# Two of the three transpose groups of a batch moved together, and both halves of a small product moved behind the last Newton step

## The chip, the cores and the metric

The kernel runs on one core of one Trainium2 chip. The metric is the device time of one execution in microseconds (us); for a kernel it is the median over its runs. The kernel before took 1432.73 us, the median of three runs between 1431.31 and 1433.15.

## What is computed

The reference chains a Nystrom attention and two feed-forward blocks. For each of 8 batches and 8 heads, with 576 positions of 64 channels, q and k are averaged over groups of 18 positions to 32 landmarks, and

```python
A = sm(q, k_lm); Bm = sm(q_lm, k_lm); C = sm(q_lm, k)     # row softmax of scaled products
Z = Bm.T / (norm1(Bm) * norminf(Bm) + 1e-06)
for _ in range(6):
    Z = 2 * Z - Z @ Bm @ Z                                # Newton steps
attn = A @ Z @ C @ v
x = ((attn @ w1) * (attn @ w2)) @ w3 @ w_out              # first block
out = elu(x @ w_in) @ w_out2                              # second block
```

The change touches only how C @ v is scheduled: the exponentials of C's scores have to be transposed before they can be multiplied with v.

## The kernel before

The work falls into three stretches. A start-up prepares the first batch and folds w3 and w_out into one matrix. Then comes the attention and first-block stretch, from about 130 to 640 us of the profile: 128 units, 16 for each of 8 batches. A last stretch computes the second block. The change lies in the middle one.

A unit `u` of batch `b` has two half steps, numbered `hs` = 0 to 31 within the batch. In each unit the loop at L915 issues, in this order: `ab(u)` (12 TensorE matmuls, L707 to L709), `quick` (the `r0` or `newton` step of the even half step, if there is one, L890), `ab_product(u)` (a ScalarE copy L716 and a VectorE product L718), the split of the product of the unit before (ScalarE L70, VectorE L71), `fill` for the even half step, `yy(u - 2)` (12 matmuls, L734 to L736), and `fill` for the odd half step. The order is written out by hand, and every engine works through its own instructions in this order.

`fill(b, hs)` runs, among other things, the attention steps of the *next* batch that the table `steps` (L522) has under `hs`. So the attention of batches 1 to 7 is computed piecewise between the matmuls of the batch before. Batch 0 has a table of its own (`first=True`) and is computed in the start-up.

The steps that matter here, for batches 1 to 7:

- `c_scores` at 7 and 8 writes the raw scores of C into two tiles `e` (128 partitions by 576, one for each half of the heads). `c_max` and `c_exp` at 9 and 10 take the maximum (VectorE L334, L335) and the exponential in place (ScalarE L338): the half 0 at 9, the half 1 at 10.
- `b_norms` at 10 and `b_norms2` at 11 prepare the Newton iteration on VectorE; `b_norms2` ends with the product at L399. `r0` at 12 (issued by `quick`) is 8 small matmuls (L406) and one VectorE product out of PSUM (L408). `newton` at 13 to 18 is six times 8 small matmuls (L418) and one VectorE operation out of PSUM (L420). Each depends on the one before.
- `c_trans` (L423) comes in three parts. Part 0 transposes four 128-column blocks of `e[0]` on TensorE (L429) into one PSUM tile, and ScalarE copies this to `ct` (L434). Part 1 does the same for `e[1]`. Part 2 transposes the last 64 columns of both halves (L432), copied by L436.
- `cv` (L438) multiplies `ct` with v, 20 matmuls (L447) for each half into one PSUM tile; after the second half VectorE scales the result into `cvbd` (L457). `zcv` at 21 (L466) multiplies it with the Newton result, and `m_tiles` (24 to 3 of the next batch, L317 with `z`) uses that. `a_scores` (22 and 26) and its steps on VectorE (L488 and on) are the other half of the attention.

All PSUM tiles of these steps come from one pool with two buffers, taken in turn:

```python
ps_at = ctx.enter_context(tc.tile_pool(name="ps_at", bufs=2, space=bass.MemoryType.PSUM))   # L243
def ps(self, nm):
    return ps_at.tile([128, 512], F32, name=f"{nm}_{self.b}", tag="at")                      # L290
```

A matmul into a new tile has to wait until the tile that last held this buffer has been read out. In the kernel before the order of tiles is, from half step 11 on: transposes 0, r0, Newton 0, transposes 1, Newton 1, Newton 2, transposes 2, Newton 3, 4, 5, cv, z.

Of the kernel before, what the change touches and what calls it, by code (L numbers as in the profile page):

```python
# [64 lines left out]
def nystrom_moe_kernel(ctx, tc, qT, kT, vm, vr, w12, w3T, w_out1, w_in2, w_out2, out):  # L65
# [216 lines left out]
    class Attention:  # L282
# [239 lines left out]
        def steps(self, first=False):  # L522

            s = {}

            def at(i, f, *a):
                s.setdefault(i, []).append((f, a))

            for hp in range(NP):
                at((-16, -14, -12, -11)[hp], self.sums, "k", hp)  # L530
                at(hp, self.sums, "q", hp)
            at(4, self.q_pad)
            lead = 2 if first else 0
            at(6 - lead // 2, self.b_scores)
            at(7 - lead // 2, self.b_exp)
            if first:
                at(7, self.b_soft)
                at(7, self.c_scores, 0)
                at(8, self.b_norms)
                at(8, self.c_scores, 1)  # L540
                at(9, self.b_norms2)
            else:
                at(7, self.c_scores, 0)
                at(8, self.c_scores, 1)
                at(8, self.b_soft)
            at(9, self.c_max, 0)
            at(9, self.c_exp, 0)
            if not first:
                at(10, self.b_norms)
            else:  # L550
                at(10, self.r0)
            at(10, self.c_max, 1)
            at(10, self.c_exp, 1)
            if not first:
                at(11, self.b_norms2)
                at(12, self.r0)
            at(17 if first else 13, self.c_norm)
            for k in range(6):
                at(13 - lead + k, self.newton, k)
            for k in range(3):  # L560
                at(11 + lead // 2 + 2 * k, self.c_trans, k)
            at(18, self.cv, 0)
            at(19, self.cv, 1)
            at(21, self.zcv)
            when = ((22, 22, 23, 24, 25, 26, 27), (26, 27, 28, 29, 30, 32, 34))
            if first:
                when = ((11, 11, 12, 13, 14, 15, 16), (17, 17, N1, N1 + 1, N1 + 2, N1 + 3, N1 + 4))
            for n, o in enumerate(when):
                at(o[0], self.a_scores, n)
                at(o[1], self.a_max)  # L570
                at(o[2], self.a_sub)
                at(o[3], self.a_exp)
                at(o[4], self.a_sum)
                at(o[5], self.a_mul, n)
                at(o[6], self.a_split, n)
            return s
# [6 lines left out]
    with tc.manual_schedule():  # L583
# [55 lines left out]
        for o in ORDER:  # L639
            if o == "A":  # L640
                k, n_wo = n_wo, n_wo + 1
# [400 lines left out]
```

## Time and profile before

| What | Value |
|---|---|
| Median of 3 runs (1431.31 to 1433.15) | 1432.73 us |
| The profiled execution: span from first to last instruction | 1430.4 us |
| Its own time beside the span | not given apart; the three runs lie 0.9 to 2.8 us above this span |
| TensorE (PE) busy | 1368.1 us, 96% |
| VectorE (DVE) busy | 1087.5 us, 76% |
| ScalarE (ACT) busy | 630.4 us, 44% |
| GpSimd (POOL) busy | 367.7 us, 26% |
| Mean granted TensorE clock | 0.988 of full speed |

PE is the matmul engine, and PEld its loads of weights, which overlap the matmuls. In a timeline a row has its start, its length, the engine, the line of the kernel, the operation, what it writes and reads, and how many neighbours were merged into it; a square bracket gives how long the engine sat idle before it and what ended that. The ends of matmuls are modelled, so the distance from one start to the next tells more than the length. An fp32 matmul leaves two records, so that 8 matmuls read x16 and 20 read x40.

### The profile page before, as it was taken

How to read it: one execution, taken by the hardware profiler on the slowest of the kernel's cores; microseconds unless marked ns; L12 is line 12 of the kernel's file. 1: busy time of each engine (PE TensorE's matmuls, PEld its weight loads, DVE VectorE, ACT ScalarE, POOL GpSimd, SP SyncE). 2: the span in 40 equal slices, each digit the busy share in tenths (PEclk: the TensorE clock that was granted, in tenths of full speed). 3: DMA queues.
4: the chain of work that ended last, by engine and by line, in shares of the span. 5: the costliest groups of instructions: out<-in, count | busy, mean ns of one | idle time of the engine just before them, and what ended most of it. 6: DMA issues, size and time to landing. Idle time of an engine off the chain costs nothing.

```text
span 1430.4 us, 27132 instructions
## 1 busy us (share of the span) xinstructions
PE 1368.1 (96%) x10848; PEld 1178.8 (82%) x10848; DVE 1087.5 (76%) x2003; ACT 630.4 (44%) x1266; POOL 367.7 (26%) x378
## 2 busy tenths in 40 slices
PE   5786999999999999999999999999999999999998
PEld 2234788888878888899999989999898998989987
DVE  7988687778687787744887878878687887878774
ACT  5534454445344545433444443544443444434442
POOL 4442336345265363420301101010110101011000
PEclk9988999999999999999999999999999999999999
DMA  8744354453535543252976464565646556555440
GB/s 306 239 139 132 109 168 164 158 179 101 203 99 195 200 136 112 93 201 81 416 259 220 155 247 173 198 221 184 224 166 222 198 185 226 193 199 192 179 159 30
DMA packets 56014, 259.70 MB, mean 182 GB/s; under 512 B 5200, under 2 KB 14416, under 8 KB 43600
## 3 DMA queue, kind: packets, MB, share of 16 engines
q0 software_dynamic: 12672, 140.51, 27.2%
q1 hardware_dynamic: 43216, 117.46, 23.7%
q8 instruction: 85, 1.39, 0.4%
q14 instruction: 41, 0.34, 0.1%
HBM read 216.01 MB, written 41.94 MB: 180 GB/s over the span
## 4 chain that ended last, share of the span: by engine, by line
PE 84%; DVE 12%; DMA 2%; ACT 1%; issue 1%; SPq 0%; DVEq 0%; ACTq 0%
PE o L873 9%; PE o L872 9%; PE o L871 9%; PE hm L812 8%; PE hm L813 8%; PE hm L814 8%; PE y L734 5%; PE ab L707 4%; PE ab L708 4%; PE ab L709 4%; PE y L736 4%; PE y L735 4%; PE m L317 2%; DVE w_b L128 1%; DVE w_b L124 1%
## 5 line engine op out<-in xcount | busy, mean ns | idle before, releaser
L812 PE MATMUL hm<-yb,wh 128*128 128x256 f32 x1008 | 285.2, 283 | 2.5 <-DVE g L830 1.7
L813 PE MATMUL hm<-yb,wh 128*128 128x256 f32 x1008 | 285.1, 283 | 0.0
L814 PE MATMUL hm<-yb,wh 128*128 128x256 f32 x1008 | 284.9, 283 | 0.0
L873 PE MATMUL o<-wo,el 128*128 128x512 f32 x576 | 225.6, 392 | 0.0
L872 PE MATMUL o<-wo,eh 128*128 128x512 f32 x576 | 225.3, 391 | 0.0
L871 PE MATMUL o<-wo,eh 128*128 128x512 f32 x576 | 224.0, 389 | 0.0
L843 ACT ACTIVATE t<-m 128x512 f32<-128x512 f32 x144 | 89.9, 624 | 299.3 <-DVE m L841 299.3
L812 PEld LDWEIGHTS hm<-yb,wh 128*128 128x128 f32 x1008 | 192.9, 191 | 5.7 <-DVE g L830 1.9
L758 POOL DMA_DIRECT2D wh<-wh_d x72 | 39.4, 548 | 611.0 <-PE hm L814 606.4
L813 PEld LDWEIGHTS hm<-yb,wh 128*128 128x128 f32 x1008 | 192.9, 191 | 2.8
L814 PEld LDWEIGHTS hm<-yb,wh 128*128 128x128 f32 x1008 | 193.0, 192 | 0.0
L734 PE MATMUL y<-gh,w3oh 128*128 128x288 f32 x512 | 160.8, 314 | 2.9 <-DVE w3ol L71 2.9
L846 DVE SCALAR_TENSOR_TENSOR t<-m,t 128x512 f32<-128x512 f32 x144 | 99.2, 689 | 77.9 <-ACT m L844 77.9
L707 PE MATMUL ab<-ath,mh 128*128 128x288 f32 x512 | 157.1, 307 | 0.0
L708 PE MATMUL ab<-atl,mh 128*128 128x288 f32 x512 | 151.9, 297 | 0.0
L709 PE MATMUL ab<-ath,ml 128*128 128x288 f32 x512 | 151.3, 295 | 0.0
L736 PE MATMUL y<-gh,w3ol 128*128 128x288 f32 x512 | 151.2, 295 | 0.0
L735 PE MATMUL y<-gl,w3oh 128*128 128x288 f32 x512 | 151.0, 295 | 0.0
L734 PEld LDWEIGHTS y<-gh,w3oh 128*128 128x128 f32 x512 | 96.3, 188 | 40.7 <-issue 22.3
L873 PEld LDWEIGHTS o<-wo,el 128*128 128x128 f32 x576 | 108.1, 188 | 22.6
L871 PEld LDWEIGHTS o<-wo,eh 128*128 128x128 f32 x576 | 108.5, 188 | 20.9
L872 PEld LDWEIGHTS o<-wo,eh 128*128 128x128 f32 x576 | 108.1, 188 | 21.2
(146 smaller groups left out, 2729.5 us busy)
## 6 DMA issues: line engine op xcount, KB each, us to landing
wh<-wh_d POOLq DMA_DIRECT2D x72, 1792.0 KB, 7.8
wo_raw<-in_w_out_dram SPq DMA_DIRECT2D x24, 512.0 KB, 5.3
k<-in_kT_dram SPq DMA_DIRECT2D x8, 1152.0 KB, 7.1
q<-in_qT_dram SPq DMA_DIRECT2D x8, 1152.0 KB, 5.2
yd<-ysb SPq DMA_DIRECT2D x16, 576.0 KB, 3.6
yin<-yd SPq DMA_DIRECT2D x9, 1024.0 KB, 9.9
out_dram<-osb SPq DMA_DIRECT2D x36, 256.0 KB, 2.3
w_raw<-in_w3T_dram SPq DMA_DIRECT2D x16, 512.0 KB, 5.1
```

What stands on the lines that cost most here:

```text
L707: pe.matmul(p[:, :NH], mh[:, cs], ah[:, blk, :], start=(blk == 0), stop=False)
L708: pe.matmul(p[:, :NH], mh[:, cs], al[:, blk, :], start=False, stop=False)
L709: pe.matmul(p[:, :NH], ml[:, cs], ah[:, blk, :], start=False, stop=(blk == 1))
L734: pe.matmul(a[oc][:, :NH], w3o_hi[fc][:, os_], gh, start=(fc == 0), stop=False)
L735: pe.matmul(a[oc][:, :NH], w3o_hi[fc][:, os_], gl, start=False, stop=False)
L736: pe.matmul(a[oc][:, :NH], w3o_lo[fc][:, os_], gh, start=False, stop=(fc == K1 - 1))
L812: pe.matmul(o, ah, bh[:, kk, :], start=(kk == 0), stop=False)
L813: pe.matmul(o, ah, bl[:, kk, :], start=False, stop=False)
L814: pe.matmul(o, al, bh[:, kk, :], start=False, stop=(kk == 1))
L871: pe.matmul(a, eh[:, ts_], w[:, 0, :], start=first, stop=False)
L872: pe.matmul(a, eh[:, ts_], w[:, 1, :], start=False, stop=False)
L873: pe.matmul(a, el[:, ts_], w[:, 0, :], start=False, stop=last)
```

## The change

For batches 1 to 7, part 0 of the transposes stays at half step 11, part 1 moves from 13 to 12, and part 2 from 15 to 12. The first half of the product with v moves from 18 to 19, where the second half already is. For batch 0 the numbers stay what they were (12, 14, 16 and 18).

```diff
             for k in range(3):
-                at(11 + lead // 2 + 2 * k, self.c_trans, k)
-            at(18, self.cv, 0)
+                at((12, 14, 16)[k] if first else (11, 12, 12)[k], self.c_trans, k)
+            at(18 if first else 19, self.cv, 0)
             at(19, self.cv, 1)
```

The order of the PSUM tiles of batches 1 to 7 becomes: transposes 0, r0, transposes 1, transposes 2, Newton 0 to 5, cv, z. On TensorE the transposes of parts 1 and 2 now stand behind the r0 matmuls and ahead of the `yy` of that unit; the 40 matmuls of `cv` stand behind the `yy` of the unit of half steps 18 and 19.

## Rows read from the trace of the kernel before

**Rows 1.** The page: its span, and the chain that ended last.
```profile
span 1430.4 us, 27132 instructions
...
PE 84%; DVE 12%; DMA 2%; ACT 1%; issue 1%; SPq 0%; DVEq 0%; ACTq 0%
```

**Rows 2.** Who waited for whom, PE: us in total, times, longest us.
```profile
PE n L418 <- DVE X L408: 4.6, 4, 1.7
PE m L317 <- DVE at L488: 3.1, 3, 2.2
PE ct L429 <- ACT e L338: 2.5, 3, 1.1
```

**Rows 3.** Timeline of PE, attention of batch 4 at half steps 12 and 13.
```profile
355.02 0.33 PE L406 MATMUL r<-bt 32*32 32x32 f32 x16
355.28 0.40 PE L734 MATMUL y<-gh,w3oh 128*128 128x288 f32 x1
...
357.96 0.43 PE L418 MATMUL n<-X 32*32 32x64 f32 x16 [0.80 <-DVE X L408]
358.31 0.66 PE L429 MATMUL ct<-ident,e 128*128 128x128 f32 x4
358.73 0.38 PE L707 MATMUL ab<-ath,mh 128*128 128x288 f32 x1
```

**Rows 4.** Timeline of ACT in the same stretch.
```profile
355.87 0.78 ACT L338 ACTIVATE e<-e,cb 128x576 f32<-128x576 f32 x1 [2.46 <-DVE cb L335]
...
356.64 0.56 ACT L434 COPY ct<-ct 128x512 f32<-128x512 f32 x1
```

**Rows 5.** Timeline of DVE there; and line 399: duration ns min/median/max.
```profile
357.69 0.21 DVE L408 TENSOR_TENSOR X<-r,brc 128x64 f32<-128x64 f32 x1
...
L399 DVE TENSOR_TENSOR X<-bm,brc x8: 224/225/1168, 63.9 to 569.1; 128x64 f32<-128x64 f32 x8
```

**Rows 6.** Timelines at the same place of batch 2 and batch 7.
```profile
217.81 0.33 PE L406 MATMUL r<-bt 32*32 32x32 f32 x16
219.44 0.56 ACT L434 COPY ct<-ct 128x512 f32<-128x512 f32 x1
...
566.68 0.33 PE L406 MATMUL r<-bt 32*32 32x32 f32 x16
568.16 0.57 ACT L434 COPY ct<-ct 128x512 f32<-128x512 f32 x1
570.14 0.21 DVE L408 TENSOR_TENSOR X<-r,brc 128x64 f32<-128x64 f32 x1
570.41 0.43 PE L418 MATMUL n<-X 32*32 32x64 f32 x16 [1.62 <-DVE X L408]
```

**Rows 7.** Timelines at the same place of batch 1.
```profile
149.20 0.59 ACT L434 COPY ct<-ct 128x512 f32<-128x512 f32 x1 [0.98 <-PE ct L429]
151.08 0.23 DVE L408 TENSOR_TENSOR X<-r,brc 128x64 f32<-128x64 f32 x1 [0.98 <-PE r L406]
```

**Rows 8.** PE timeline rows; and the stretch 393.25 to 396.66 (PEclk behind POOL's share).
```profile
382.69 1.09 PE L317 MATMUL m<-w_sb,z 64*32 64x512 f32 x16
393.35 2.32 PE L317 MATMUL m<-w_sb,z 64*32 64x512 f32 x16 [2.16 <-DVE at L488]
...
393.25:396.66 3.41, 3.31 (x20) 1.47 (x21) 3.13 (x8) 2.27 (x6) 1.42 (x1) 0.50 0.02 5
...
148.50 0.66 PE L429 MATMUL ct<-ident,e 128*128 128x128 f32 x4 [2.18 <-DVE ml L479]
```

**Rows 9.** Timelines of PE and DVE, batch 4, half steps 19 to 21.
```profile
372.09 0.90 PE L447 MATMUL cv<-v,ct 128*32 128x64 f32 x40
373.06 1.24 DVE L457 TENSOR_TENSOR cvbd<-cv,crs 32x128 f32<-32x128 f32 x4 [1.74 <-PE cv L447]
...
376.29 0.66 PE L466 MATMUL z<-X,cvbd 128*64 128x32 f32 x16
```

**Rows 10.** Who waited for whom, DVE, 120 to 640 us: total, times, longest.
```profile
DVE X L420 <- PE n L418: 30.2, 24, 2.3
```

## Prediction

> **What bounds the kernel now.** I read the page first. The span is 1430.4 us, and the chain that ended last lies on PE for 84% and on DVE for 12% of it [rows 1]: in the long run the matmul engine sets the pace, so an edit matters if it changes how much PE does or how long PE stands still. Next I read the list of waits for PE in the middle stretch [rows 2]. PE stands still seldom there, and one of the entries lies exactly where the change is made: Newton step 0 waits for the DVE product that reads r0 out of PSUM, 4 times, 4.6 us together. Then I took the timelines of the three engines around half step 12 of one batch, and looked for what the moved transposes would find there: the PE rows [rows 3], the ACT rows [rows 4], the DVE rows [rows 5]. The reader should see in them that PE comes to the end of r0 at 355.28, before three things that the moved transposes need are done.
>
> **What the change removes and adds on PE: nothing.** Each part of the transposes keeps its matmuls, its own PSUM tile and its ACT copy. Part 1 takes PE 0.42 us (358.31 to 358.73 [rows 3]), wherever it stands. Before, parts 1 and 2 stood right behind a Newton step; after, they stand right behind r0. So the number of places where PE changes from large matmuls to small ones and back stays the same, and no gain comes from fewer groups. The same holds for `cv`: its first half stood right behind Newton step 5, its second half by itself; after, the Newton step stands by itself and both halves together. I count both moves of PE work as 0.
>
> **cv, half step 18 to 19.** The second half ends where it ended before, since both orders put the same matmuls ahead of it. Its readers don't come later: DVE scales the result from 373.06 to 374.30, and PE wants it only at 376.29 [rows 9], so 2 us are left. The ACT copies of `yy` that fall in this unit start up to 0.9 us earlier (the length of one half [rows 9]) and nobody waits for them there. Cost 0; if that cover were gone, it could be at most the 0.9 us of one half in each batch. No DMA is issued in any of these steps, and none is passed on a DMA queue by moving them: v, the only loaded tile they read, is replaced two units after `cv` as before (L927, in the unit of half steps 22 and 23).
>
> **Transposes 1 and 2 behind r0.** They need three things there.
> - The exponentials of half 1. Their ACT instruction starts at 355.87 and takes 0.78 [rows 4], so it ends at 356.65, while r0 leaves PE at 355.28.
> - For part 1, the PSUM buffer of part 0, as two buffers are taken in turn. ACT copies that tile only behind the exponential: 356.64 plus 0.56 is 357.20 [rows 4]. This is the later one.
> - For part 2, the buffer of r0, read out by DVE at 357.69 plus 0.21, 357.90 [rows 5].
>
> PE works in order, so the 12 matmuls of `yy` behind the transposes, which need none of this, wait too, and behind them Newton 0 and the next `ab`. Before, this `yy` was the cover: it ran for 2 us while ACT and DVE caught up.
>
> For batch 4: the start after a wait comes 0.06 us behind its releaser (357.90 to 357.96 [rows 3, 5]). So part 1 starts at 357.26, a wait of 1.98 us after 355.28. It takes 0.42, to 357.68. Part 2 starts at 357.96, a wait of 0.28. What goes is the wait of Newton 0, 0.80 [rows 3], since by then the DVE product is long done. Net 1.98 + 0.28 - 0.80 = 1.46 us.
>
> The other batches by the same rows. Batch 2: r0 leaves PE at 217.81 + 0.26 = 218.07, the copy ends at 220.00 [rows 6], wait 1.99; DVE is early, and Newton 0 did not wait before; net 1.99. Batch 7: 566.94, the copy ends at 568.73, wait 1.85; part 1 runs from 568.79 to 569.21, the DVE product ends at 570.35, wait 1.20; gone is 1.62 [rows 6]; net 1.43. Between them the pattern repeats: batch 3 gives 1.87 + 1.22 - 1.66 = 1.43, batch 5 1.99 - 0.47 = 1.52, batch 6 1.98. Batch 1 has nothing to wait for: its copy ended at 149.79, and its DVE product itself waited for PE, ending at 151.31 [rows 7], while part 1 runs on PE. Batch 0 isn't changed. The sum: 14.36 us of new waits, less the 4.55 at Newton 0 (the 4.6 of [rows 2]), is **9.8 us**.
>
> DVE sets some of these times. The product at line 399, just ahead of r0's, took between 0.224 and 1.168 us [rows 5]. Long in the batches where it was short, it would add 1.4 us to the sum (0.29 + 0.86 + 0.28 in batches 2, 5, 6); short where it was long, it would take off the second waits, 2.7 us (1.22 + 0.28 + 1.20). It follows other work ahead of the change, so I take it as it was and keep both ends.
>
> **The clock.** After one wait of 2.16 us PE ran at a granted clock of 0.50, the lower of its two levels (1.2 of 2.4 GHz), for a stretch of 3.41 us, and the m matmuls took 2.32 instead of 1.09 us; half of 3.41 is 1.7 us lost [rows 8]. After another wait, of 2.18 us, the transposes took their usual 0.66, so the clock held [rows 8]. After 1.62 us the Newton matmuls took 0.43 us, as after 0.80 [rows 3, 6]: no loss there either. The new waits are 1.85 to 2.0 us in six batches, and in batches 3 and 7 they come to 3.1 us with only 0.42 us of work between. The ends are thus none, or less by the one loss there is now (-1.7), and six losses (10.2). I take two, for batches 3 and 7, whose waits are longer than the one that lost the clock: 3.4 us. The Trainium skill, "TensorE: Matmul & The Clock Gate", section "Why this matters for your kernels", warns only of gaps longer than any single one of these; by that advice the term is 0 and the sum 9.8. The trace disagrees: 2.16 us sufficed once.
>
> **Sum.** 9.8 + 3.4 = 13.2 us. The durations are those of the profiled execution, span 1430.4; its own time isn't given apart, and the median of the runs is 2.3 us above its span. I take that remainder as unchanged: 1432.7 + 13.2 = **1445.9 us**, 0.9% slower.
>
> **Rivals.** What can be told from no change in this kernel is about 0.2%, 2.9 us.
> - *A, no clock lost* (22%). The waits come as above, but the transposes between them and the shortness of each keep the clock. For it: the 2.18 us wait [rows 8], and the advice above. Time: 1432.7 + 9.8 = 1442.5.
> - *B, clock lost in most batches* (15%). Four or more of six: 9.8 + 4 x 1.7 = 16.6, 1449.3, and with long DVE products up to 1451.
> - *C, the waits are only moved forward* (5%). PE reaches all later waits of a batch 1.4 to 2 us later, so DVE and ACT could be ahead there and those waits vanish: 3.1 us before the m matmuls and 2.5 before the first transposes [rows 2], and with the first the clock loss of 1.7. Then 9.8 - 7.3 = 2.5 us are left, 1435.2, no change that can be told. It decides if DVE carries its lead over the half batch between. Against it: DVE waits for PE at the Newton steps right behind, 24 times, 30.2 us [rows 10], so its lead is used up there. It is the case on the other side of my forecast.
> - *D, the edit has no effect on the order* (3%): the steps are in the table, but another order comes out on PE, and the time is that of before. If the transposes took fewer changes of shape on PE than I count, this would be the place for a small gain, under 0.3 us a batch.
>
> **Numbers.** The forecast has 55%. The range from 1440.5 to 1451.0 holds it with A and B: at the low end the waits without a clock loss and some of the 2.7 us of DVE taken off, at the high end four losses and 1.4 us of DVE added. Outside are C, D and extremes, some 15%. Slower by over 0.2%: 0.92; within: 0.06; faster: 0.02.
>
> **What would show it.** In the new list of waits PE should have transposes waiting for the ACT copy at line 434 (about 11.7 us in six batches) and for the DVE product at line 408 (2.7 us in three), and Newton 0 waiting for nothing. Stretches right behind should show a clock of 0.5 in about two batches. The cv matmuls should show no wait, and z none on `cvbd`. It is wrong if PE goes from r0 into the transposes without idle time, or if waits before the m matmuls go by as much as the new ones come.

## The result, and the profile after

The changed kernel takes 1449.93 us, the median of four runs (1445.66 to 1454.11), against 1432.94 for the kernel before in the same comparison: 17.0 us more, a ratio of 1.0123 with a 95% interval from 1.0107 to 1.0139. Here and below, a ratio and its interval are estimated from the single runs of a comparison; they aren't quotients of the two medians, and differ from those by up to 0.001. The forecast was 1445.9 with a range from 1440.5 to 1451.0.

The page of the kernel after, its span and the chain that ended last. The profiled execution is one of the long ones, 1453.69 us:

```profile
span 1451.9 us, 27130 instructions
...
PE 83%; DVE 13%; DMA 2%; ACT 1%; issue 1%; SPq 0%; DVEq 0%; ACTq 0%
```

Against [rows 1], the share of DVE in the chain has gone from 12% to 13%. Who waited for whom, PE in the middle stretch of the kernel after: total, times, longest, in us:

```profile
PE ct L429 <- DVE X L408: 15.4, 6, 3.5
PE m L317 <- DVE at L488: 2.8, 2, 2.2
PE ct L429 <- ACT e L338: 2.4, 3, 1.1
```

Against [rows 2], the wait of Newton 0 for line 408 (4.6 us, 4 times) has gone, and in its place the transposes wait 15.4 us, in six batches, for the same product of line 408. The two other entries have hardly moved: 2.8 for 3.1 and 2.4 for 2.5. So 10.8 us of waits at these lines are new, and none of them is won back later.

Batch 4 of the kernel after, PE:

```profile
361.07 0.33 PE L406 MATMUL r<-bt 32*32 32x32 f32 x16
364.07 1.08 PE L429 MATMUL ct<-ident,e 128*128 128x128 f32 x4 [2.67 <-DVE X L408]
364.95 0.63 PE L432 MATMUL ct<-ident,e 128*64 128x128 f32 x2
365.23 0.59 PE L734 MATMUL y<-gh,w3oh 128*128 128x288 f32 x1
...
368.39 0.65 PE L418 MATMUL n<-X 32*32 32x64 f32 x16
```

and ACT and DVE there:

```profile
362.69 0.57 ACT L434 COPY ct<-ct 128x512 f32<-128x512 f32 x1
...
363.71 0.21 DVE L408 TENSOR_TENSOR X<-r,brc 128x64 f32<-128x64 f32 x1
```

In [rows 3] the `yy` matmuls started 0.26 us behind r0; here they start at 365.23, 4.16 us behind it. The reader should see two more things. Part 1 of the transposes starts 0.15 us behind the end of the DVE product (363.92), and not behind the ACT copy of part 0, which ended at 363.26. And the rows behind the wait are long: the four transposes read 1.08 instead of 0.66 us, Newton 0 reads 0.65 instead of 0.43. That is the clock, in the view of stretches (length, busy time of PE, PEld, DVE, ACT and POOL, then the granted clock):

```profile
362.50:369.30 6.80, 5.23 (x35) 4.73 (x36) 2.52 (x9) 2.81 (x8) 1.21 (x1) 0.55 0.94 305
```

A granted clock of 0.55 over the stretch is the lower of the two levels (1.2 GHz) for nearly all of it. The mean clock over the whole span is 0.981, and that of the profile before 0.988. What waits and clock cost is read from the same view of the whole middle stretch, from the first `ab` to the last `yy`, for the kernel before and the one after:

```profile
118.39:671.50 553.11, 535.75 (x5687) 464.80 (x5680) 400.97 (x884) 249.00 (x593) 227.19 (x218) 0.99 0.41 142
```

```profile
118.82:691.50 572.68, 543.55 (x5687) 471.99 (x5680) 402.08 (x884) 248.54 (x593) 227.41 (x218) 0.98 0.39 137
```

PE runs the same number of instructions (5687) in both. It stands idle for 17.4 us before and 29.1 after, 11.8 more (the 10.8 above, and 1 us at other lines), and the same work keeps it busy for 7.8 us longer, which is the lower clock. Together they are 19.6 of the 21.5 us by which the spans differ; 0.4 more lie ahead of this stretch and 1.5 behind it, where the clock was at the lower level once (701.14 to 704.55 us). The four runs of the first comparison show the same in their times: the two near 1454 us had a clock of 0.981, the two near 1446 us one of 0.988.

Batch 1, where I had expected no wait, has none; and `cv` runs in one piece, the 40 matmuls as 80 records, and in the middle stretch PE waits neither at `cv` nor at `zcv` for its result (timeline of PE):

```profile
151.51 0.66 PE L429 MATMUL ct<-ident,e 128*128 128x128 f32 x4
...
166.71 1.73 PE L447 MATMUL cv<-v,ct 128*32 128x64 f32 x80
```

### The profile page after: what moved, and what is told of

The parts are those of the page before. It is cut to its first block, busy times and chain, and to the rows that moved or that the text cites. A ratio compares the mean times of both kernels' runs of the same rounds, so it can differ in the third digit from the quotient of the medians.

```text
span 1451.9 us, 27130 instructions
## 1 busy us (share of the span) xinstructions
PE 1377.5 (95%) x10848; PEld 1187.7 (82%) x10848; DVE 1088.7 (75%) x2003; ACT 630.3 (43%) x1266; POOL 367.8 (25%) x378
## 4 chain that ended last, share of the span: by engine, by line
PE 83%; DVE 13%; DMA 2%; ACT 1%; issue 1%; SPq 0%; DVEq 0%; ACTq 0%
PE o L873 9%; PE o L872 9%; PE o L871 9%; PE hm L812 8%; PE hm L813 8%; PE hm L814 8%; PE y L734 5%; PE ab L707 4%; PE y L736 4%; PE y L735 4%; PE ab L708 4%; PE ab L709 4%; PE m L317 2%; DVE w_b L128 1%; PE n L418 1%
## 5 line engine op out<-in xcount | busy, mean ns | idle before, releaser
L716 ACT COPY a<-ab 128x288 f32<-128x288 f32 x128 | 51.3, 401 | 187.6 <-PE ab L709 187.5
L871 PEld LDWEIGHTS o<-wo,eh 128*128 128x128 f32 x576 | 108.5, 188 | 20.9
```

The costliest lines, as they stand in the source:

```text
L871: pe.matmul(a, eh[:, ts_], w[:, 0, :], start=first, stop=False)
```

## The experiments

The theory: PE reaches the transposes behind r0 before DVE has read r0 out, and stands still; that and the clock it loses are the whole price. The main rivals: `cv` carries a part; the grouping itself is dear or saves something; the waits are only moved.

**cv alone.**

```diff
-            at(18, self.cv, 0)
+            at(18 if first else 19, self.cv, 0)
```

> Only the first half of cv moves from half step 18 to 19; the transposes stay where they were. Theory (all of the price is the wait of the transposes right behind r0): the time of the kernel before within 0.2%, PE waits at line 418 for line 408 still 4.6 us in 4 times, no wait at the cv matmuls. Rival (the later first half of cv is late for its readers): several us more, with z waiting for cvbd or yy waiting behind it.

Measured: 1433.11 us against 1432.62, ratio 0.9999 (0.9991 to 1.0008). The waits of PE in the middle stretch:

```profile
PE n L418 <- DVE X L408: 4.5, 4, 1.6
PE m L317 <- DVE at L488: 3.2, 3, 2.2
PE ct L429 <- ACT e L338: 2.3, 3, 1.1
```

They are those of the kernel before. This half of the change shows no cost and no gain, to within 0.1%.

**The transposes alone.**

```diff
-                at(11 + lead // 2 + 2 * k, self.c_trans, k)
+                at((12, 14, 16)[k] if first else (11, 12, 12)[k], self.c_trans, k)
```

> Only the transposes move (parts at 11, 12, 12); cv stays at 18 and 19. Theory: the whole price of the change, +11 us of waits and 1.7 us for each added stretch at the lower clock, so +12 to +21 us, with transposes waiting for line 408 about 15.4 us in 6 times. Rival (cv carries a part): clearly less than the whole change in the same comparison.

Measured: 1448.68 us, ratio 1.0113 (1.0099 to 1.0126). The transposes wait for line 408 as in the change:

```profile
PE ct L429 <- DVE X L408: 15.5, 6, 3.5
```

The whole change in the same comparison had 1.0106 (1.0090 to 1.0121), so the transposes carry all of it, as far as these intervals tell.

**The change again, unaltered.**

> The changed kernel once more, unaltered. Theory (part of its time is TensorE clock lost at random): single times spread from 1445 to 1454 us, in steps of about 1.7 us, with equal waits (15.4 us in 6 times at the transposes) and a mean granted clock that falls as the time rises, 0.988 near 1446 and 0.981 near 1454. Rival (the waits themselves differ from run to run): a low time shows shorter waits at an equal clock.

Measured: 1447.73 us, ratio 1.0106; single times 1444.91, 1447.66, 1447.80 and 1448.47 with clocks of 0.988, 0.987, 0.987 and 0.985. The shortest was the profiled one. Its waits of PE, and its span with the mean clock:

```profile
PE ct L429 <- DVE X L408: 15.4, 6, 3.5
```

```profile
core 0: 1443.1 us, clock 0.988
```

The waits of the transposes are equal to a tenth with those of the execution that took 8.8 us longer. What differs is PE's busy time over the same work in the middle stretch, 538.25 us here and 543.55 there, and 2 us ahead of that stretch:

```profile
116.81:683.70 566.89, 538.25 (x5687) 467.53 (x5680) 401.90 (x884) 248.38 (x593) 227.28 (x218) 0.99 0.40 138
```

The equal mean clock of 0.988 doesn't mean that no clock was lost by the change. Between 140 us and the end of the middle stretch the kernel before was at the lower level once, behind the m matmuls' wait at 393.35 us [rows 8]; this execution was twice, right behind the long waits of batches 3 and 7:

```profile
288.83:292.24 3.41, 3.05 (x14) 3.01 (x15) 1.19 (x6) 1.41 (x3) 0.00 (x0) 0.50 0.58 178
578.97:582.38 3.41, 2.99 (x13) 2.95 (x14) 1.25 (x6) 1.41 (x3) 0.06 (x1) 0.50 0.61 189
```

Ahead of 140 us it was at that level for 3.4 us less than the kernel before, and so the mean is the same. The middle stretch is 13.8 us longer than before: 11.3 of idle time and 2.5 of busy time. The start-up was 1.6 us shorter and the end 0.5 longer, which gives the 12.7 us between the spans. The steps of 1.7 us that I had expected are not to be seen in four times.

**Both groups behind Newton 0.** The same two groups and the same `cv` as in the change, one half step later:

```diff
-                at(11 + lead // 2 + 2 * k, self.c_trans, k)
-            at(18, self.cv, 0)
+                at((12, 14, 16)[k] if first else (11, 13, 13)[k], self.c_trans, k)
+            at(18 if first else 19, self.cv, 0)
```

> Two groups of transposes as in the change, and cv as in the change, but parts 1 and 2 stand together behind Newton step 0 (11, 13, 13), after the yy that follows r0. Theory: no wait for r0's read-out beyond the old 4.6 us at Newton 0; part 2 may wait 0.4 to 0.9 us a batch for a buffer that Newton 0 or part 1 has just filled, so +0 to +6 us, no long wait and no added stretch at the lower clock. Rival (the grouping itself is dear, wherever it stands): +10 us or more as in the change. Rival (grouping saves changes of shape on PE): below the kernel before.

Measured: 1435.54 us against 1432.62, ratio 1.0029 (1.0020 to 1.0037). The waits of PE that touch these steps:

```profile
PE n L418 <- DVE X L408: 4.1, 3, 1.7
...
PE ct L432 <- ACT ct L434: 1.4, 2, 0.7
PE ct L432 <- DVE X L420: 1.2, 4, 0.6
```

Two groups in another place cost 2.9 us, and 2.6 of it stand in the lines of part 2: with two PSUM buffers it now follows two other tiles at once and waits until Newton 0 or part 1 has been read out. So the grouping isn't dear by itself, and no saving by it shows either; the place makes the price.

**Part 2 alone behind r0.**

```diff
-                at(11 + lead // 2 + 2 * k, self.c_trans, k)
+                at((12, 14, 16)[k] if first else (11, 13, 12)[k], self.c_trans, k)
```

> The kernel before with part 2 of the transposes alone moved behind r0 (11, 13, 12), the two smallest matmuls of the three groups; part 1 and cv stay. Theory (the price is that whatever stands first behind r0 waits for r0's read-out): nearly the whole price of the change, +9 to +20 us, with the wait now at line 432 and some 15 us long in 6 times. Rival (the price is that of part 1, its four matmuls and its copy): less than +4 us.

Measured: 1448.62 us against 1432.09, ratio 1.0112 (1.0097 to 1.0126). The wait has moved to line 432 with its size kept:

```profile
PE ct L432 <- DVE X L408: 14.9, 6, 3.4
```

Two matmuls that keep PE busy for less than 0.3 us (364.95 to 365.23 above, at the lower clock) carry the whole price if they are the ones that stand first behind r0. It is not the work of part 1, and not that there are two groups: here there are three.

**The change with the norms earlier.** VectorE's preparation of the Newton iteration moves from half steps 10 and 11 to 9 and 10, so that r0 is read out sooner:

```diff
-                at(10, self.b_norms)
+                at(9, self.b_norms)
...
-                at(11, self.b_norms2)
+                at(10, self.b_norms2)
```

> The changed kernel with b_norms and b_norms2 one half step earlier (9 and 10), so that the VectorE work ahead of r0's read-out is done sooner; the products themselves are the same. Theory: r0's read-out comes 1 to 2.5 us earlier and the wait behind r0 shrinks from 15.4 us to what the exponentials of half 1 and the copy of part 0 leave, 5 to 11 us, and the time falls by as much, to 1434 to 1442 us. Rival (read-out isn't what the transposes wait for): wait and time as in the change.

Measured: 1435.48 us against 1432.09, ratio 1.0021 (1.0012 to 1.0030). The waits of the transposes (the entry for line 338 includes the old one of part 0, 2.5 us in [rows 2]):

```profile
PE ct L429 <- ACT ct L434: 3.4, 4, 0.9
PE ct L429 <- ACT e L338: 3.1, 3, 1.4
...
PE ct L429 <- DVE X L408: 1.5, 2, 0.8
...
PE ct L432 <- DVE X L408: 1.3, 2, 1.0
```

By a change on DVE alone this version is 12 to 14 us faster than the change. Not all of that is the transposes' price, since the same edit is worth 4 us to the kernel before (the trial of it below): with the norms earlier in both, the transposes still cost some 7 us (1435.48 against 1428.26, from two comparisons), where they cost 15 to 17. What is late next shows up at once: the copy of part 0 on ACT and the exponentials.

A second thing differs here. In four of the six batches part 1 now waits for the copy at line 434 and starts before r0 is read out, in the buffer of part 0, as in batch 3:

```profile
285.37 0.66 PE L429 MATMUL ct<-ident,e 128*128 128x128 f32 x4 [0.78 <-ACT ct L434]
285.83 0.21 DVE L408 TENSOR_TENSOR X<-r,brc 128x64 f32<-128x64 f32 x1
```

That alone explains little, by an estimate: with this buffer and DVE as late as before, the prediction's sum has 14.4 us of new waits, against the 15.4 measured in the change.

**Newton later.** From the kernel before, an attempt to take out the waits that were there already:

```diff
-                at(13 - lead + k, self.newton, k)
+                at(13 - lead + k if first else 14 + k, self.newton, k)
...
-                at(11 + lead // 2 + 2 * k, self.c_trans, k)
+                at((12, 14, 16)[k] if first else (12, 14, 16)[k], self.c_trans, k)
```

> The kernel before with the Newton steps of batches 1 to 7 one half step later (14 to 19) and the three groups of transposes at 12, 14 and 16. Theory (what costs is PE arriving at r0's read-out and at the exponentials before they are done): the 4.6 us before Newton 0 and the 2.5 us before the first transposes go, nothing new waits, so about 7 us less than before, 1424 to 1428 us. Rival (waits only move to a later place): within 0.2% of before, with new waits at the Newton steps, z or the m matmuls.

Measured: 1431.61 us against 1432.09, ratio 0.9995 (0.9986 to 1.0003): my theory missed here, and the rival holds, though the new waits stand at `ab`, which it had not named. The waits for lines 408 and 338 are gone (7.1 us), and so is that of batch 1 for line 479 (2.2 us, [rows 8]). These are new:

```profile
PE ab L707 <- ACT a L716: 3.7, 4, 1.3
...
PE ab L707 <- DVE g L718: 2.3, 3, 1.0
...
PE ab L707 <- ACT mh L478: 1.4, 1, 1.4
```

They are 7.4 us against the 9.3 that went (0.9 us of the first stands in other versions too, the one with cv alone among them). In the batch with the longest of them (timelines of ACT and PE), the ACT copy that reads `ab` out stands behind an exponential that itself waited for its maximum on DVE:

```profile
349.98 0.78 ACT L338 ACTIVATE e<-e,cb 128x576 f32<-128x576 f32 x1 [3.76 <-DVE cb L335]
350.75 0.38 ACT L716 COPY a<-ab 128x288 f32<-128x288 f32 x1
351.18 0.40 PE L707 MATMUL ab<-ath,mh 128*128 128x288 f32 x1 [1.34 <-ACT a L716]
```

PE has come earlier to the next `ab`, whose PSUM bank isn't read out yet. So there PE is held by a chain on DVE and ACT, and moving PE's own work moved most of the wait to another place.

**The norms earlier, in the kernel before,** with nothing else changed (the edit of the norms above):

> The kernel before with b_norms and b_norms2 one half step earlier (9 and 10) and nothing else changed. Theory (in the stretch of half steps 9 to 13 PE is held by a chain of VectorE and ScalarE work, and the norms fit into VectorE's idle time behind the first maximum): the 4.6 us before Newton 0 go, and the time falls by up to that, 1427 to 1432 us. Rival (the norms only push the maximum of half 0 or the products of ab further back): within 0.2% or slower, with waits of ab for line 716 or 718 in their place, as with the later Newton steps.

Measured: 1428.26 us against 1432.27, ratio 0.9973 (0.9964 to 0.9982). The wait of Newton 0 is down from 4.6 us, and the one for line 479 in batch 1 from 2.2 to 1.2:

```profile
PE n L418 <- DVE X L408: 1.1, 2, 0.9
```

**Both together,** later Newton steps and earlier norms:

> The later Newton steps and transposes (14 to 19; 12, 14, 16) together with the earlier norms (9 and 10). Theory: with the norms out of the way the waits of ab for lines 716, 718 and 478, 7.4 us with the later Newton steps alone, shrink, and the time falls below the kernel before, 1425 to 1430 us. Rival (ab waits because the exponentials stand ahead of its copy on ScalarE, and the norms don't matter to that): waits of ab as before, 1430 to 1433 us.

Measured: 1427.62 us, ratio 0.9969 (0.9958 to 0.9981). `ab` still waits 4.0 us for line 716, as the rival has it, while its waits for lines 718 and 478 fell from 3.7 to 0.7. The two versions with earlier norms beat both kernels, by 4 to 5 us against the one before and, across comparisons, by 19 to 22 against the change; which of the two is better these runs don't tell.

## Why the prediction was right, point by point

**No gain from fewer groups: right, as far as shown.** cv alone gave 0.9999, and two groups behind Newton 0 gave no time below the kernel before.

**PE stands still behind r0, and the `yy` behind it no longer covers the lag: right.** The waits are in six batches, none in batch 1, and the wait of Newton 0 is gone, as forecast. The trial with part 2 alone shows that the price doesn't hang on which part stands there; the trial with the norms earlier shows that DVE's lateness is the larger part of the reason.

**The size of the waits: 9.8 forecast, 10.8 measured** (15.4 less 4.6). The step that was off is "For part 1, the PSUM buffer of part 0, as two buffers are taken in turn", which the description of the kernel before says too. In batches 2 to 7 part 1 waited for r0's buffer itself, so the waits for the copy at line 434 that were to show it (about 11.7 us) didn't come. Batch 2 shows it (timelines of ACT, DVE and PE): part 1 starts behind r0's read-out and 0.10 us before the copy out of part 0's buffer ends, at 220.68, so it can't be writing there.

```profile
220.12 0.56 ACT L434 COPY ct<-ct 128x512 f32<-128x512 f32 x1
220.21 0.22 DVE L408 TENSOR_TENSOR X<-r,brc 128x64 f32<-128x64 f32 x1
...
220.58 0.63 PE L429 MATMUL ct<-ident,e 128*128 128x128 f32 x4 [1.75 <-DVE X L408]
```

The trace of the kernel before showed it already. In turn, Newton 0 would stand in part 0's buffer; but in batch 2 it starts at 219.85, and the copy out of that buffer ends at 220.00 [rows 6]:

```profile
219.85 0.42 PE L418 MATMUL n<-X 32*32 32x64 f32 x16
```

A line of the view by source line, before and after, agrees with it: at line 429 the queue of PE had 7 separate semaphore instructions and has 13, six more for six batches:

```profile
L429 PEldq EVENT_SEMAPHORE  x7: 51/51/51, 77.4 to 562.2; - x7
...
L429 PEldq EVENT_SEMAPHORE  x13: 51/51/51, 77.7 to 585.8; - x13
```

Where DVE was late, part 1 could therefore not run in the meantime, as I had it between 568.79 and 569.21 for batch 7: one wait of up to 3.5 us instead of two with 0.42 us of work between. Where DVE was early, the wait came out shorter than forecast (1.75 instead of 1.99 in batch 2). The two errors partly cancel: 0.2 us too much in each of two batches, 0.3 to 0.4 too little in each of four. Why these batches get the buffers the other way round than batch 1 was not tried, and stays open.

**The clock: two lost stretches, 3.4 us, forecast; two in one profiled execution, more in the other.** The forecast put them behind batches 3 and 7, as their waits were the longest, and there they lie in the profile of the kernel taken again and in that of the transposes alone. In the long profile batches 4 and 5 lost the clock as well, and so did the wait before the m matmuls, as it had before the change. In PE's busy time of the middle stretch that is 2.5 us in the one and 7.8 in the other. So the case forecast (1445.9) and rival B (four or more batches, 1449.3 and more) were not two cases of which one is true: the kernel has both among its executions, from 1444.91 to 1454.11 us, and its median depends on how many of each kind are drawn, 1449.93 in the first comparison and 1447.73 in the second. That 1449.93 lies at rival B's time and not nearer to the forecast is the luck of such a draw: two of its four executions were long ones, and none of the four in the second comparison. Rival A (1442.5, no loss) is in no profile of the change, and no single time of it is as low.

In the row of one wait of 2.16 us [rows 8] the comparison of 2.32 with 1.09 us gives the clock too much: the same m matmuls behind the same wait took 1.45 us at full clock in the kernel taken again, so 0.87 us of that step are the clock.

The advice of the Trainium skill ("TensorE: Matmul & The Clock Gate", section "Why this matters for your kernels") is against long gaps between bursts of matmuls, and the prediction applied it to waits of at most 2 us. The measured waits of batches 3 and 7 are as long as the gaps that it names, and the losses there agree with it. Those behind 2.67 and 2.32 us, and behind 2.16 us before the m matmuls, came after shorter gaps than the Trainium skill names in that section.

**Rival C, the waits only move forward: wrong for this change.** The waits before the m matmuls are 2.8 us after 3.1. But its mechanism exists in the same stretch: later Newton steps lost 9.3 us of waits and found 7.4 others. DVE and ACT lie behind just ahead of r0, up to half step 12, and no longer behind it.

**Rival D, no effect on the order: wrong,** by the rows of batch 4 above.

## What to carry to other kernels

When work is moved on an engine that works in order, ask of every PSUM buffer it takes who read it last and when; the independent matmuls that stood between were the cover of that read, and a group of less than 0.3 us in front of them made PE wait 1.7 to 3.4 us each time. If the wait of an engine ends with another engine, move the late engine's work forward: a half step on VectorE gave 4 us here, while moving PE's own work gave nothing or only changed the place of the wait. Waits of 2 to 3.5 us on PE had a second price here in the clock, and between 2 and 3 us it varied between executions, so compare such kernels by several runs, read the granted clock beside each time, and read it by stretch, since a mean over the span also counts the start-up.

## What was not expected of the hardware

The same instructions with the same waits at the transposes took 1444.91 us in one execution and 1453.69 in another, with mean granted clocks of 0.988 and 0.981. Four profiles have the six waits behind r0: the changed kernel's two, the transposes alone, and part 2 alone. In them the clock fell to its lower level (0.50 granted) in or right behind these waits as follows; in the long profile the four transposes behind such a wait took 0.97 to 1.09 us, against 0.63 where it held.

| Batches | Waits in the four profiles | Clock at the lower level behind the wait |
|---|---|---|
| 2 and 6 | 1.66 to 1.76 us | none of 8 |
| 4 and 5 | 2.23 to 2.67 us | 4 of 8 |
| 3 and 7 | 3.38 to 3.48 us | all 8 |

The wait of 2.16 us before the m matmuls goes with the middle row: the clock fell behind it in the profiles before and after, and held in the one taken again. What decides between executions for a wait of this length these runs don't show.
